# BigBird attention and a swish layer: row-tiled scores, a 0/1 mask product, channels-first AV, row sums by matmul, q and k turned by DMA, in an order written out by hand

## Chip, cores and metric

The kernel runs on one core of a Trainium2 chip. The metric is the device time of one execution in microseconds (us), the median over runs. The engines are TensorE (PE in the profile, its weight loads PEld), VectorE (DVE), ScalarE (ACT), GpSimd (POOL) and SyncE (SP), which here only issues DMAs. SBUF is the on-chip memory, PSUM the memory that TensorE writes its results to, DRAM the memory off the core. Each engine takes its own instructions in program order.

## What is computed

Block-sparse attention over 4 batches, 8 heads, 768 positions and 64 channels, followed by a feed-forward layer (512 to 2048 to 512) on the 3072 tokens:

```python
scores = scale * np.matmul(q, k.transpose(0, 1, 3, 2))
mask = np.abs(blk_i - blk_j) <= window            # blocks of 32, window 1
mask = mask | (blk_i == 0) | (blk_j == 0) | (blk_i == n_blocks - 1) | (blk_j == n_blocks - 1)
...  # and three sampled key blocks per query block
scores = np.where(mask, scores, -1000000000.0)
attn = np.exp(scores - np.max(scores, axis=-1, keepdims=True))
attn = attn / (np.sum(attn, axis=-1, keepdims=True) + 1e-09)
x = np.matmul(attn, v)            # then [B, S, H*D] -> [3072, 512]
h = x @ w_in
out = (h * (1.0 / (1.0 + np.exp(-beta * h)))) @ w_out
```

## The kernel before

**Units of work.** Heads are taken in pairs (`j` = 0 to 3 in each batch `b`). The queries are cut into eight tiles of 256 or 512 columns (`tiles`, L329), and the tiles into seven groups (`groups`, L331) of 256 or 512 tokens. For every tile and pair the attention is computed with keys on the partitions and queries along the row; when a group's tiles are done, its tokens go through the feed-forward layer.

**Loading** (`emit_load` L65). SP issues one plain load each for k, q and v of a pair, 384 KB in fp32, two pairs ahead. Position `s` lies on partition `s // 6`, so a partition reads 1536 contiguous bytes per head. The weights come as eight DMAs on POOL's queue (L143, L147), which cast fp32 to fp16 on the way.

**Preparation** (`emit_prep` L196). VectorE casts k and q to fp16 (L204), TensorE turns each in six 128x128 transposes (L209), and VectorE copies the two heads out of PSUM into four tiles `kA`, `qA`, `kB`, `qB` (L213, L214). The mask sits in the contraction: 24 extra rows hold a one-hot of the block on the key side and 0 or -30000 per block on the query side (L185 to L190), so that a score matmul of 88 rows (head A) or 128 rows (head B) gives masked scores at once. v is cast into `va` with a column of ones (L217).

**Scores and exp** (`step` L227). Per head, two or three key chunks of 128 are multiplied (L234) into a PSUM tile `sc` (two buffers), and ScalarE takes exp of 1024 or 768 columns at a time into `et` (L240): 160 such instructions in all.

**AV** (`av_step` L250). For each 128 queries and each key chunk, 128 columns of `et` are loaded as weights and the 65 columns of `va` stream through (L260): 1152 matmuls, which give queries on the partitions and the row sum in column 64. VectorE takes the reciprocal (L265) and multiplies (L266) into `xst`; TensorE turns that back to channels-first (L274) and VectorE copies it into `xT_sb` (L276).

**Feed-forward** (`moe_steps` L284). A group has 16 `h_step`s, each four matmuls `hp` (L294), a tanh on ScalarE (L299) and a product on VectorE into `g` (L301); then per 128 tokens four `o_step`s of four 512-column matmuls `op` (L313), with the last one's result scaled by ScalarE into `osb` (L318) and stored by SP (L322). `hp`, `op`, `tp` and `xtp` share the three PSUM buffers `mm`.

**Order.** The program order is a list of attention steps per group, with the previous group's feed-forward steps (the backlog) spread evenly between them (L371 to L383); the framework's scheduler may move instructions from that order. A tile's AV steps come after the second score step of the pair that follows.

Of the kernel before, what the change touches and what calls it, by code (L numbers as in the profile page):

```python
# [17 lines left out]
def kernel(  # L18
# [19 lines left out]
    N_TOK = B * S  # L38
# [4 lines left out]
    VW = D + 2  # L43
    NEG = -30000.0

    persist = ctx.enter_context(tc.tile_pool(name="persist", bufs=1))
    stage_pool = ctx.enter_context(tc.tile_pool(name="stage", bufs=3))
    et_pool = ctx.enter_context(tc.tile_pool(name="et", bufs=14))
    work_pool = ctx.enter_context(tc.tile_pool(name="work", bufs=3))
    g_pool = ctx.enter_context(tc.tile_pool(name="g", bufs=2))  # L50


    NVA = 6
    va_tiles = []
    for i in range(NVA):
        va = persist.tile([P, 2, NC, VW], FP16, name=f"va_{i}")
        nc.gpsimd.memset(va[:, :, :, D:VW], 1.0)
        va_tiles.append(va)

    def pair_src(x, b, j):  # L60
        return x[b, 2 * j:2 * j + 2].rearrange("h (p c) d -> p h (c d)", c=NC)

    loaded = {}

    def emit_load(b, j):  # L65
        sts = []
        for name, src in (("k", k), ("q", q), ("v", v)):
            st32 = stage_pool.tile([P, 2, NC * D], FP32, tag=f"{name}st", name=f"{name}st")
            nc.sync.dma_start(out=st32, in_=pair_src(src, b, j))
            sts.append(st32)  # L70
        loaded[(b, j)] = sts

    identity = persist.tile([P, P], FP16, name="identity")

    emit_load(0, 0)
    make_identity(nc, identity)
    ident32 = persist.tile([P, P], FP32, name="ident32")
    nc.gpsimd.tensor_copy(out=ident32[0:16, 0:16], in_=identity[0:16, 0:16])


# [4 lines left out]
    nc.scalar.dma_start(out=sb_i32, in_=sb_lo)  # L85
    beta_sb = persist.tile([N_FFC, P], FP32, name="beta_sb")
    nc.scalar.dma_start(out=beta_sb, in_=moe_beta.rearrange("(c p) -> c p", p=P))

    sb_f32 = persist.tile([NB, 3], FP32, name="sb_f32")
    nc.vector.tensor_copy(out=sb_f32, in_=sb_i32)  # L90


# [10 lines left out]
    onehot = persist.tile([NB, NC, P], FP16, name="onehot")  # L103
    nc.gpsimd.memset(onehot, 1.0)
    nc.gpsimd.affine_select(out=onehot, in_=onehot, pattern=[[1, NC], [NC, P]],
                            compare_op=ALU.is_ge, fill=0.0, base=0,
                            channel_multiplier=-BLK)
    nc.gpsimd.affine_select(out=onehot, in_=onehot, pattern=[[-1, NC], [-NC, P]],
                            compare_op=ALU.is_ge, fill=0.0, base=BLK - 1,
                            channel_multiplier=BLK)  # L110

    mask_blk = persist.tile([NB, NB], FP32, name="mask_blk")
# [3 lines left out]
    for val in (0.0, float(NB - 1)):  # L116
        nc.vector.scalar_tensor_tensor(out=mask_blk, in0=iota_j, scalar=val, in1=mask_blk,
                                       op0=ALU.is_equal, op1=ALU.max)
        nc.vector.scalar_tensor_tensor(
            out=mask_blk, in0=iota_i[:, 0:1].to_broadcast([NB, NB]), scalar=val,  # L120
            in1=mask_blk, op0=ALU.is_equal, op1=ALU.max)
    for r in range(3):
        nc.vector.scalar_tensor_tensor(out=mask_blk, in0=iota_j, scalar=sb_f32[:, r:r + 1],
                                       in1=mask_blk, op0=ALU.is_equal, op1=ALU.max)
    mask16 = persist.tile([NB, NB], FP16, name="mask16")
    nc.vector.tensor_scalar(out=mask16, in0=mask_blk, scalar1=1.0, scalar2=-NEG,  # L126
                            op0=ALU.subtract, op1=ALU.mult)
    oh_flat = onehot.rearrange("j c p -> j (c p)")


    xT_sb = persist.tile([P, NPAIR, N_TOK], FP16, name="xT_sb")
    w_in_sb = persist.tile([P, NPAIR, D_FF], FP16, name="w_in_sb")
    w_out_sb = persist.tile([P, N_FFC, D_MODEL], FP16, name="w_out_sb")
    beta_h_sb = persist.tile([P, N_FFC], FP32, name="beta_h_sb")

    w_in_r = moe_w_in.rearrange("(c p) f -> p c f", p=P)
    w_out_r = moe_w_out.rearrange("(c p) m -> p c m", p=P)

    def gate(w, like):
        nc.gpsimd.tensor_copy(out=w[0:1, 0, 0:1], in_=like[0:1, 0, 0:1])  # L140

    def emit_w_in(i):
        nc.gpsimd.dma_start(out=w_in_sb[:, :, i * 512:(i + 1) * 512],  # L143
                            in_=w_in_r[:, :, i * 512:(i + 1) * 512])

    def emit_w_out(i):
        nc.gpsimd.dma_start(out=w_out_sb[:, i * 4:(i + 1) * 4, :],  # L147
                            in_=w_out_r[:, i * 4:(i + 1) * 4, :])


    sc_pool = ctx.enter_context(
        tc.tile_pool(name="sc_psum", bufs=2, space=bass.MemoryType.PSUM))
    av_pool = ctx.enter_context(
        tc.tile_pool(name="av_psum", bufs=1, space=bass.MemoryType.PSUM))
    mm_pool = ctx.enter_context(
        tc.tile_pool(name="mm_psum", bufs=3, space=bass.MemoryType.PSUM))

    NSET = 5  # L160
    sets = []
    for i in range(NSET):
        four = {}
        for nm in ("kA", "qA", "kB", "qB"):
            four[nm] = persist.tile([P, S], FP16, name=f"{nm}_{i}")
        nc.gpsimd.memset(four["kB"][0:D, :], 0.0)
        nc.gpsimd.memset(four["qB"][0:D, :], 0.0)
        sets.append(four)

    maskx_box = {}  # L170

    def emit_mask():
        ps = mm_pool.tile([P, 512], FP32, tag="mm", name="bet")
        nc.tensor.transpose(out=ps[:, 0:N_FFC], in_=beta_sb, identity=ident32[0:16, 0:16])
        nc.vector.tensor_scalar(out=beta_h_sb, in0=ps[:, 0:N_FFC], scalar1=0.5,
                                scalar2=None, op0=ALU.mult)
        maskx = persist.tile([NB, S], FP16, name="maskx")
        for lo, hi in ((0, 512), (512, S)):
            ps = mm_pool.tile([P, 512], FP32, tag="mm", name="mkx")
            nc.tensor.matmul(ps[0:NB, 0:hi - lo], lhsT=mask16, rhs=oh_flat[:, lo:hi],  # L180
                             start=True, stop=True)
            nc.vector.tensor_copy(out=maskx[:, lo:hi], in_=ps[0:NB, 0:hi - lo])
        maskx_box["m"] = maskx

    def emit_set(i):  # L185
        four, maskx = sets[i], maskx_box["m"]
        nc.vector.tensor_copy(out=four["qA"][D:D + NB, :], in_=maskx)
        nc.gpsimd.tensor_copy(out=four["kA"][D:D + NB, :], in_=oh_flat)
        nc.vector.tensor_copy(out=four["qB"][0:NB, :], in_=maskx)
        nc.gpsimd.tensor_copy(out=four["kB"][0:NB, :], in_=oh_flat)  # L190


    prepared = {}
    n_prep = [0]

    def emit_prep(b, j):  # L196
        kst, qst, vst = loaded.pop((b, j))
        four = sets[n_prep[0] % NSET]
        if n_prep[0] < NSET:
            emit_set(n_prep[0])  # L200
# [216 lines left out]
```

The softmax here doesn't subtract the row's maximum and nothing guards it: scores larger than these inputs give would overflow.

## Time and profile before

| | value |
|---|---|
| median of 3 runs | 339.46 us (339.13 to 339.80) |
| span of the profiled execution | 337.4 us |
| PE busy, matmuls | 298.4 us, 2659 |
| ACT busy | 215.8 us |
| DVE busy | 181.7 us |
| POOL busy | 28.0 us |
| DMA written | 29.78 MB, 20880 packets |
| granted TensorE clock, mean | 0.998 |

The span runs from the first to the last instruction of the profiled execution; the median of the runs is 2.1 us above it. A busy time is the union of an engine's instructions, not their sum. Matmuls are pipelined: the mean duration of one 512-column matmul in the page is 379 ns, while 32 in a row take 7.07 us, 0.22 us from one to the next.

### The profile page before, as it was taken

The numbers are of one execution on the slowest core, as the hardware profiler recorded it, in microseconds if no ns is written. First come the engines' busy times: TensorE is split into PE (matmuls) and PEld (weight loads), VectorE is DVE, ScalarE is ACT, GpSimd is POOL, SyncE is SP. The second block draws the span as 40 slices with busy tenths as digits, with TensorE's granted clock in tenths as the row PEclk, the third lists the DMA queues.
The fourth block names the chain that finished last, engine by engine and source line by source line (L and its number), as shares of the span: only waits on it lengthen the run. The fifth ranks groups of instructions, "written<-read, shape, count | busy, mean of one in ns | idle before, by whom it ended". The sixth has DMA issues, their size and how long they took to land.

```text
span 337.4 us, 6399 instructions
## 1 busy us (share of the span) xinstructions
PE 298.4 (88%) x2659; PEld 172.2 (51%) x2659; DVE 181.7 (54%) x408; ACT 215.8 (64%) x297; POOL 28.0 (8%) x48
## 2 busy tenths in 40 slices
PE   0055589999999999999999999999999999999995
PEld 0034466655555555555566445455455455555662
DVE  3989764543787451557866366115667114561360
ACT  1011389985998545978554989665986756954561
POOL 9994000000000000000000000000000000000000
PEclk9999999999999999999999999999999999999999
DMA  7999994112530340021340000011000010001101
GB/s 242 384 228 225 267 330 179 50 47 80 161 97 11 123 130 33 31 79 64 96 157 31 33 0 2 31 38 58 1 3 0 33 62 33 0 2 62 64 2 62
DMA packets 20880, 29.78 MB, mean 88 GB/s; under 512 B 1380, under 2 KB 17780, under 8 KB 20852
## 3 DMA queue, kind: packets, MB, share of 16 engines
q1 hardware_dynamic: 16512, 25.17, 21.8%
q0 software_dynamic: 4224, 4.19, 7.5%
q8 instruction: 21, 0.34, 0.4%
q14 instruction: 7, 0.06, 0.1%
q10 hardware_dynamic: 116, 0.01, 0.0%
HBM read 27.27 MB, written 6.29 MB: 99 GB/s over the span
## 4 chain that ended last, share of the span: by engine, by line
PE 64%; DVE 16%; ACT 14%; issue 4%; DMA 2%; SPq 0%; ACTq 0%; DVEq 0%
PE op L313 23%; PE hp L294 16%; PE sc L234 12%; PE av L260 9%; ACT et L240 8%; ACT t_sb L299 6%; DVE g L301 4%; PE tp L209 2%; PE xtp L274 2%; DMA qst<-in_q_dram 2%; DVE q_203 L204 1%; DVE va_70 L217 0%; DVE xst L266 0%; DVE qB_157 L214 0%; DVE qB_139 L214 0%
## 5 line engine op out<-in xcount | busy, mean ns | idle before, releaser
L240 ACT ACTIVATE et<-sc 128x1024 f16<-128x1024 f32 (+1 forms) x160 | 146.8, 953 | 80.4 <-PE sc L234 80.2
L313 PE MATMUL op<-w_out_sb,g 128*128 128x512 f16 x384 | 97.0, 379 | 0.1
L294 PE MATMUL hp<-xT_sb,w_in_sb 128*128 128x512 f16 (+1 forms) x448 | 95.6, 348 | 1.0 <-DVE g L301 0.2
L301 DVE SCALAR_TENSOR_TENSOR g<-t_sb,hp 128x512 f16<-128x512 f16 (+1 forms) x112 | 67.1, 610 | 44.9 <-ACT t_sb L299 44.4
L299 ACT ACTIVATE t_sb<-hp,beta_h_sb 128x512 f16<-128x512 f32 (+1 forms) x112 | 69.8, 653 | 12.1 <-PE hp L294 10.9
L294 PEld LDWEIGHTS <-w_in_sb 128*128 128x128 f16 x448 | 42.2, 97 | 35.9 <-issue 1.9
L260 PEld LDWEIGHTS <-et 128*128 128x128 f16 x1152 | 44.2, 99 | 21.6 <-DVE xst L266 10.4
L313 PEld LDWEIGHTS <-g 128*128 128x128 f16 x384 | 34.9, 97 | 33.2 <-DVE qB_163 L214 0.4
L265 DVE RECIPROCAL recip<-av 128x2 f32<-128x2 f32 (+1 forms) x64 | 11.2, 176 | 70.3 <-PE av L260 70.0
L318 ACT ACTIVATE osb<-op 128x512 f32<-128x512 f32 x24 | 14.3, 598 | 23.2 <-PE op L313 19.7
L266 DVE TENSOR_TENSOR xst<-av,recip 128x128 f16<-128x128 f32 (+1 forms) x64 | 22.8, 357 | 1.6
L276 DVE COPY xT_sb<-xtp 128x256 f16<-128x256 f16 (+1 forms) x32 | 11.5, 358 | 14.6 <-PE xtp L274 14.6
L274 PEld LDWEIGHTS <-xst 128*128 128x128 f16 x96 | 6.4, 97 | 12.5 <-DVE xst L266 12.2
L260 PE MATMUL av<-va_70,et 128*128 128x65 f16 x216 | 9.6, 199 | 2.8 <-DVE xst L266 2.7
L234 PE MATMUL sc<-qB_139,kB_138 128*128 128x256 f16 (+1 forms) x48 | 11.6, 344 | 0.5 <-ACT et L240 0.5
L274 PE MATMUL xtp<-identity,xst 128*128 128x128 f16 x96 | 10.9, 222 | 1.0 <-DVE xst L266 0.9
L234 PE MATMUL sc<-qA_137,kA_136 88*128 88x256 f16 (+1 forms) x48 | 11.1, 344 | 0.5 <-ACT et L240 0.3
L180 PE MATMUL mkx<-onehot,mask_121 24*24 24x512 f16 (+1 forms) x2 | 0.8, 506 | 10.3 <-DVE mask_121 L126 10.3
L260 PE MATMUL av<-va_72,et 128*128 128x65 f16 x216 | 9.5, 196 | 0.0
L234 PE MATMUL sc<-qB_145,kB_144 128*128 128x256 f16 (+1 forms) x36 | 8.8, 348 | 0.9 <-ACT et L240 0.9
L234 PE MATMUL sc<-qA_143,kA_142 88*128 88x256 f16 (+1 forms) x36 | 8.7, 350 | 0.6 <-ACT et L240 0.6
L234 PE MATMUL sc<-qB_163,kB_162 128*128 128x512 f16 (+1 forms) x36 | 8.5, 325 | 0.7 <-ACT et L240 0.7
(206 smaller groups left out, 249.4 us busy)
## 6 DMA issues: line engine op xcount, KB each, us to landing
kst<-in_k_dram SPq DMA_DIRECT2D x16, 384.0 KB, 4.7
qst<-in_q_dram SPq DMA_DIRECT2D x16, 384.0 KB, 5.5
vst<-in_v_dram SPq DMA_DIRECT2D x16, 384.0 KB, 5.4
out_dram<-osb SPq DMA_DIRECT2D x24, 256.0 KB, 2.0
w_in_sb<-in_moe_w_in_dram POOLq DMA_DIRECT2D x4, 512.0 KB, 10.1
w_out_sb<-in_moe_w_out_dram POOLq DMA_DIRECT2D x4, 512.0 KB, 21.7
sb_i_95<-in_sampled_blocks_dram ACTq DMA_DIRECT2D x1, 0.3 KB
beta_sb<-in_moe_beta_dram ACTq DMA_DIRECT2D x1, 8.0 KB, 4.5
```

The lines of the kernel that those rows point to most:

```text
L234: nc.tensor.matmul(sc[:, i * n:(i + 1) * n], lhsT=kx[0:rows, (kc0 + i) * P:(kc0 + i + 1) * P], rhs=qx[0:rows, q0:q0 + n], start=True, stop ...
L240: nc.scalar.activation(out=et[:, 0:kn * n], in_=sc[:, 0:kn * n], func=AF.Exp, bias=0.0, scale=SCALE)
L260: nc.tensor.matmul(av[:, qc, :], lhsT=et[:, i * n + qc * P:i * n + (qc + 1) * P], rhs=va[:, hh, kc, 0:D + 1], start=(kc == 0), stop=(kc == ...
L265: nc.vector.reciprocal(out=recip[:, 0:nq], in_=av[:, 0:nq, D])
L266: nc.vector.tensor_tensor(out=xstage[:, 0:nq, hh * D:(hh + 1) * D], in0=av[:, 0:nq, 0:D], in1=recip[:, 0:nq].to_broadcast([P, nq, D]), op= ...
L274: nc.tensor.transpose(out=xtp[:, qc, :], in_=xstage[:, qc, :], identity=identity)
L276: nc.vector.tensor_copy(out=xT_sb[:, j, b * S + q0:b * S + q0 + n], in_=xtp[:, 0:nq, :].rearrange("p c s -> p (c s)"))
L294: nc.tensor.matmul(hp[:, 0:n], lhsT=w_in_sb[:, c, f * P:(f + 1) * P], rhs=xT_sb[:, c, t0:t0 + n], start=(c == 0), stop=(c == NPAIR - 1))
L299: nc.scalar.activation(out=t_sb[:, 0:n], in_=hp[:, 0:n], func=AF.Tanh, bias=0.0, scale=beta_h_sb[:, f:f + 1])
L301: nc.vector.scalar_tensor_tensor(out=g[:, f, 0:n], in0=t_sb[:, 0:n], scalar=1.0, in1=hp[:, 0:n], op0=ALU.add, op1=ALU.mult)
L313: nc.tensor.matmul(op, lhsT=g[:, f, ts * P:(ts + 1) * P], rhs=w_out_sb[:, f, :], start=(f == 0), stop=(f == N_FFC - 1))
L318: nc.scalar.activation(out=osb, in_=op, func=AF.Copy, bias=0.0, scale=0.5)
```

## The change

Nearly the whole kernel is rewritten around the same tiles and groups. The reader needs these parts:

- The framework's scheduler is off (`manual_schedule`); every engine's order is the program's.
- k and q are cast to fp16 by DMAs from DRAM to DRAM on POOL's queue (`emit_load`), in an order where one row holds both heads' 64 channels of a position, then turned by a DMA transpose on SP's queue into `kT` and `qT` (128 channels of a pair by 768 positions, `emit_turn`). v is cast by a DMA into `va`. The first four pairs and the eight weight DMAs are issued one after the other on POOL's queue.
- The mask is a tile `mask01` of 0 and 1 (keys by queries), built once; VectorE multiplies it into `et` after the exp, leaving out the first and last query block, for which every key is allowed.
- Score matmuls contract 64 rows: head 0 in the upper half of the array, head 1 in the lower, each into a PSUM bank of its own. An exp always covers 1024 columns.
- AV has v as weights (64 columns a head) and streams `et`: head 0 gives partitions 0 to 63, head 1 gives 64 to 127, so the result is channels-first.
- Row sums are matmuls with ones as weights, 32 columns of the array for each of four heads (a "couple" is two pairs). VectorE takes the reciprocals, and five DMAs on SP's queue write them to DRAM and read them back, broadcast over 64 partitions each, into `rb`. One VectorE product then writes `xt`.
- The output's scaling moves from ScalarE to VectorE.
- The order: 144 score steps; a couple's sums come 2 steps after its last score step, its AV products 8 and 9 steps after; a group's feed-forward steps are appended one step later and fed at 1.28 us of estimated TensorE work a step (`PACE`), as long as there are any.

```diff
+    ctx.enter_context(tc.manual_schedule())
...
-    et_pool = ctx.enter_context(tc.tile_pool(name="et", bufs=14))
+    kq_pool = ctx.enter_context(tc.tile_pool(name="kq", bufs=6))
+    et_pool = ctx.enter_context(tc.tile_pool(name="et", bufs=26))
...
+        k16 = dram_pool.tile([S, 2, D], FP16, tag="k16", name="k16")
+        q16 = dram_pool.tile([S, 2, D], FP16, tag="q16", name="q16")
+        va = kq_pool.tile([P, 2, NC, D], FP16, tag="va", name="va", bufs=8)
+        for src, dst in ((k, k16), (q, q16)):
+            nc.gpsimd.dma_start(out=dst.rearrange("s h d -> h s d"), in_=src[b, 2 * j:2 * j + 2])
+        nc.gpsimd.dma_start(
+            out=va.rearrange("p h c d -> p (h c) d"),
+            in_=v[b, 2 * j:2 * j + 2].rearrange("h (c p) d -> p (h c) d", p=P))
...
+        for st, dst in ((k16, kT), (q16, qT)):
+            nc.sync.dma_start_transpose(out=dst.unsqueeze(1),
+                                        in_=st.rearrange("s h d -> s (h d)"))
...
+    mask01 = persist.tile([P, NC, S], FP16, name="mask01")
+    for c in range(NC):
+        ps = sc_pool.tile([P, 1024], FP32, tag="sc", name="mk")
...
+    def couple(b, q0, n, j0, xt_off, xt_key):
+        kn = 512 // n
...
+                sc = sc_pool.tile([P, 2, kn, n], FP32, tag="sc", name="sc")
                 for i in range(kn):
+                    for hh in range(2):
+                        nc.tensor.matmul(
+                            sc[:, hh, i, :],
+                            lhsT=kT[hh * D:(hh + 1) * D, (kc0 + i) * P:(kc0 + i + 1) * P],
+                            rhs=qT[hh * D:(hh + 1) * D, q0:q0 + n],
+                            start=True, stop=True)
+                et = et_pool.tile([P, 2, kn, n], FP16, tag="et", name="et")
+                nc.scalar.activation(out=et, in_=sc, func=AF.Exp, bias=0.0, scale=SCALE)
+                lo = BLK if q0 == 0 else 0
+                hi = n - BLK if q0 + n == S else n
                 for i in range(kn):
+                    m = mask01[:, kc0 + i, q0 + lo:q0 + hi]
+                    nc.vector.tensor_tensor(
+                        out=et[:, :, i, lo:hi], in0=et[:, :, i, lo:hi],
+                        in1=m.unsqueeze(1).to_broadcast([P, 2, hi - lo]), op=ALU.mult)
...
+        def sums():
+            dt = av_pool.tile([P, 512], FP32, tag="av", name="dsum")
+            for h in range(nh):
+                for kc in range(NC):
+                    for t in range(4):
+                        nc.tensor.matmul(
+                            dt[32 * t:32 * t + 32, 0:256],
+                            lhsT=sel[:, h, :] if nh == 2 else ones32,
+                            rhs=ets[(t // 2, t % 2, kc)][:, h * 256:(h + 1) * 256],
+                            start=(h == 0 and kc == 0), stop=(h == nh - 1 and kc == NC - 1))
+            r = work_pool.tile([P, 256], FP32, tag="recip", name="recip")
+            for x in range(2):
+                nc.vector.reciprocal(out=r[:, x * 128:(x + 1) * 128],
+                                     in_=dt[:, x * 128:(x + 1) * 128])
+            dr = dram_pool.tile([P, 256], FP32, tag="dr", name="dr")
+            nc.sync.dma_start(out=dr, in_=r)
...
+                    nc.sync.dma_start(out=rb[hh * D:(hh + 1) * D, 0:n],
+                                      in_=src.to_broadcast([D, n]))
...
+        def av(jj):
...
+                at = av_pool.tile([P, 512], FP32, tag="av", name="av")
+                for kc in range(NC):
+                    for hh in range(2):
+                        nc.tensor.matmul(at[hh * D:(hh + 1) * D, 0:n],
+                                         lhsT=va[:, hh, kc, :],
+                                         rhs=ets[(jj, hh, kc)],
                                          start=(kc == 0), stop=(kc == NC - 1))
+                nc.vector.tensor_tensor(out=xt[:, j0 + jj, xt_off:xt_off + n],
+                                        in0=at[:, 0:n], in1=box["rb"][jj][:, 0:n],
+                                        op=ALU.mult)
...
-                    nc.scalar.activation(out=osb, in_=op, func=AF.Copy, bias=0.0, scale=0.5)
+                    nc.vector.tensor_scalar(out=osb, in0=op, scalar1=0.5, scalar2=None,
+                                            op0=ALU.mult)
...
+    LAG_S, LAG_A0, LAG_A1 = 2, 8, 9
...
+    PACE = 1.28
+    def feed(amount):
+        acc = amount + feed.left
+        while backlog and acc >= backlog[0][0] * 0.5:
+            c, fn = backlog.pop(0)
+            fn()
+            acc -= c
+        feed.left = acc if backlog else 0.0
...
+        while n_turned < len(seq) and first_use[n_turned] <= x + 7:
+            emit_turn(n_turned)
+            n_turned += 1
+            if n_turned >= 3 and n_loaded < len(seq):
+                emit_load(n_loaded)
+                n_loaded += 1
...
+        feed(PACE if x < n_steps else 1.0)
```

## The prediction

> **What bounds the kernel now.** I read the page's busy times and slices first, then the chain of waits, the groups by shape, and last the timeline of the tail.
>
> ```profile
> PE 298.4 (88%) x2659; PEld 172.2 (51%) x2659; DVE 181.7 (54%) x408; ACT 215.8 (64%) x297; POOL 28.0 (8%) x48
> ...
> PE   0055589999999999999999999999999999999995
> ...
> ACT  1011389985998545978554989665986756954561
> ...
> PE 64%; DVE 16%; ACT 14%; issue 4%; DMA 2%; SPq 0%; ACTq 0%; DVEq 0%
> ```
>
> TensorE is idle or half idle for 45 us and then busy to the end. The stretch from 100 to 300 us, in equal windows (columns: busy time of PE, PEld, DVE, ACT, POOL), leaves it 3.7 of 200 us:
>
> ```profile
> 100.00:150.00 50.00, 48.54 (x444) 27.06 (x441) 25.86 (x58) 35.38 (x47) 0.00 (x0) 1.00 0.21 70
> 150.00:200.00 50.00, 48.76 (x457) 28.45 (x456) 31.89 (x76) 35.38 (x49) 0.00 (x0) 1.00 0.21 69
> 200.00:250.00 50.00, 49.30 (x420) 25.85 (x420) 23.87 (x50) 36.85 (x48) 0.00 (x0) 1.00 0.06 22
> 250.00:300.00 50.00, 49.70 (x405) 26.55 (x403) 22.86 (x46) 35.97 (x50) 0.00 (x0) 1.00 0.06 22
> ```
>
> Busy is not the same as streaming, so the chain is asked for the true spacing: 32 output matmuls take 6.92 us, 0.216 us for 512 columns, 0.108 for 256.
>
> ```profile
> 326.58 6.92 PE op L313 x32
> ```
>
> So TensorE bounds the kernel, at its streaming rate, and ScalarE is next at 36 of 50 us. The rows that price the rest:
>
> ```profile
> L240 ACT ACTIVATE et<-sc 128x1024 f16<-128x1024 f32 x96 | 97.0, 1046 | 28.9 <-PE sc L234 28.7
> L299 ACT ACTIVATE t_sb<-hp,beta_h_sb 128x512 f16<-128x512 f32 x80 | 55.3, 710 | 10.3 <-PE hp L294 9.2 <-DVE recip L265 1.0
> L301 DVE SCALAR_TENSOR_TENSOR g<-t_sb,hp 128x512 f16<-128x512 f16 x80 | 54.1, 686 | 34.2 <-ACT t_sb L299 33.8
> L301 DVE SCALAR_TENSOR_TENSOR g<-t_sb,hp 128x256 f16<-128x256 f16 x32 | 13.0, 421 | 10.7 <-ACT t_sb L299 10.6
> 14.90 3.15 POOL L143 DMA_DIRECT2D w_in_sb<-in_moe_w_in_dram  x4
> ```
>
> **TensorE's work, part by part.** Removed: by line, the AV matmuls (48.6 us busy), the q/k transposes (16.7) and the transposes back (10.9), 76 us. Scores before: 192 x 0.216 + 192 x 0.108 = 62.2 us. Feed-forward: 704 x 0.216 + 128 x 0.108 = 165.9, unchanged. New: the scores have the same columns in 384 half-height matmuls; run two at a time, 31.1 us. AV has as many columns, two at a time 31.1. Sums: 576 matmuls of 256 columns, four at a time, 15.6. Total 243.7 for 298.4. Whether tiles overlap no row of before shows; the ends are full overlap (243.7) and none (165.9 + 3 x 62.2 = 352.5). I take full overlap, because score tiles have rows and banks of their own and AV tiles columns of their own; the other end is a rival.
>
> **A cost between tiles.** TensorE now alternates each step between tiled and whole-array matmuls. A 512-column matmul lasts 379 ns (page) but its successor starts after 216: if the array empties at a switch, that costs up to 163 ns, else 0, so two switches add 0 to 0.33 us a step. The Trainium skill speaks against this change here: TensorEngine Tiling (Array Packing), section Tiling Modes, says a change of tiling mode, not of tile, drains the engine. By that rule the upper end would hold, which would add some 32 us over 98 mixed steps if TensorE set all of them; without it nothing. The rows say only what an emptying could cost; I use their middle.
>
> **ScalarE.** 144 exps of 1024 (1.01 us each, 97.0 / 96) = 145, tanh 69.8, outputs gone (14.3 us moves): about 215, unchanged.
>
> **VectorE.** Removed by line: casts 21.4 and 9.3, copies 17.6, 17.9 and 5.3, reciprocals 11.2, normalising 22.8, copy back 11.5: 117 us. Left: g 67.1. Added: outputs 24 x 0.686 = 16.5; `xt` 16 x 0.686 + 16 x 0.421 = 17.7; reciprocals: 128x2 takes 170 ns and 128x4 182, so 6 ns an element, 0.93 us for 128, 32 of them 29.8 (0.29 each at the 1.04 ns an element of the g rows, so 9 to 30; I take 30, the row of the same operation). The mask product: g's two rows give 1.04 ns an element and 0.157 fixed, so 960 elements cost 1.15 us at one a cycle; the fp16 copies `kA` (768 elements in 550 ns, fixed part taken off) run at 0.51 ns, so 0.65 us. A wide tile takes 96 of 960, a narrow one 96 of 448 (0.39 or 0.62 us): 100 or 170 us. All operands are fp16 in SBUF, as the fast row's are 16 bit, so I take 100. Total 231, from 181.7.
>
> **The steps.** TensorE a step: scores 0.216, AV and sums 46.7 / 144 = 0.32, feed-forward 1.28: 1.82. Feed-forward's first half (hp) needs 1.5 tanh of 0.69 beside an exp: ScalarE 1.01 + 1.04 = 2.05; VectorE 0.65 + (2 x 0.93 + 2 x 0.69) / 12 + 1.5 x 0.68 = 1.94, in narrow tiles 2.2. The second half (op) is TensorE's, 1.82 to 2.15. I take 1.96 for both (1.82 to 2.1). A step without feed-forward is ScalarE's, 1.01.
> How many of each: tiles end at steps 12, 36, 60, 72, 84, 108, 132, 144, and a group's work is there 10 steps after its last tile. It lasts 13.7 / 1.28 = 10.7 steps for 256 tokens, 27.4 / 1.28 = 21.4 for 512. So after step 12: 10 steps bare, 10.7 fed, 13.3 bare, four times 21.4 fed and 2.6 bare, 2 fed. Fed 98.3 x 1.96 = 192.7; bare 33.7 x 1.01 = 34.0. Then ten positions of 1.0 us of feeding plus some 0.3 of sums and AV, 13; then 27.4 - 2.6 - 10 = 14.9 of the sixth group, and the last as now: hp three in 1.62 us (timeline of the tail), 8.6, op 7.0, last output and its store 3.9: 34.4. Sum 274.
>
> **The start.** Scores now begin at 21.7 us behind VectorE's casts. After the change q of pair 3 is the eleventh DMA on POOL's queue, and step 9 needs it. POOL needs 0.79 us for a DMA of 512 runs (row above); one load has 1536: 0.8 (by instruction) to 2.4 us (by run). In the packet records a 512-byte packet takes 27 ns and a 1536-byte one 65, so 256 bytes some 18; the cast 2048-byte ones take 98. With 96 packets an engine: 1.7 to 9.4 us a load. I take 2.4. So 1 + 11 x 2.4 = 27.4, landing 2.0 (output stores' row), the transpose, then three steps. The transpose has no row: 2.0 by that store, 55 us if each 2-byte element cost a 9 ns packet on 16 engines; its runs are 256 bytes, nearest to the loads (384 KB land in 4.7), so 4. Step 12 ends at 36 (29 with 1.7 and 2.0; 113 with 9.4). The Trainium skill, DMA: Bandwidth & Descriptors, Specifications, asks for 512 bytes or more, below which the engine reads, modifies and writes; these write 128. If that doubled the 2.4, step 12 would end at 63.
>
> **The new wait.** From sums to `rb`: sums 1.3, reciprocals 1.9, store 0.4 + 2.0, four loads 1.6 + 2.0 (issue 0.4 each, landing as the stores): 9.2 us. The window is six steps: 11.8 fed, but 6.1 bare. Some four couples come late by up to 3 us; `xt` then stands at the head of VectorE's queue with mask products and g behind it, for which sums and op matmuls wait. I add 5 (0 to 12). A late turn on SP's queue would hold these DMAs too.
>
> **Sum.** 36 + 274 + 5 = 315 against a span of 337.4; with the 2.1 us between span and median, **317 us**.
>
> **Rivals.**
> - *Everything overlaps, no switch costs:* 29 + 34 + 98.3 x 1.82 + 13 + 34.4 = 289, so 291. For it: TensorE streams without gaps now. Against: three engines within 10% of each other and only three `mm` buffers.
> - *The q/k path starves the start (slower):* place, POOL's queue before step 9. The gain after it is 22 us, so it decides from 11 x (r - 2.4) = 22, r = 4.4 us a load, 46 ns a packet. At the cast row's 98 ns, 9.4 us, 48 loads alone take 451 us, so some 450 to 480. For it: a DRAM target and 128-byte pieces, of which no row exists. Against: 18 ns by the small rows.
> - *Mask product at one element a cycle:* bare steps 1.42 for 1.01 (+14), hp steps 2.43 for 1.96 (49 x 0.47 = +23): 354.
> - *Tiles don't overlap (the change doesn't do what it says):* 0.43 three times a step, 2.57 for 1.96 in 98 fed steps (+60), +10 in the bare ones: 387.
> - *Upper ends of switch and late `rb`:* 98.3 x 0.14 + 7 = +21: 338, about none to slightly slower.
>
> **How the numbers follow.** Forecast (300 to 337) 0.44; full overlap 0.15; no change 0.02; q/k path 0.15; mask 0.08; no overlap 0.07; upper ends and beyond 0.09. Below 0.2%, 0.7 us, a measurement of this kernel can't tell a difference. Faster 0.59, same 0.02, slower 0.39. The range, 291 to 362, takes in full overlap and the slow mask product, and leaves out most of the q/k and no-overlap cases, 0.19 with a little below. The forecast's own is 300 to 337.
>
> **What would show it.** Right: PE busy near 245 to 275; score matmuls in pairs that start together; the mask group near 650 ns at 960 elements; first scores near 15 us, step 12 near 36; ScalarE above 85% in hp stretches. Wrong: score idle time released by the transposes' DMAs; mask product near 1.15 us; VectorE busy above 270; `xt` with long idle before it released by `rb`; sum matmuls spaced 0.1 us apart instead of four together.

## The result, and the profile after

| | before | after |
|---|---|---|
| median | 339.29 us (339.0 to 339.8) | 665.09 us (663.66 to 667.51, 4 runs) |
| ratio, 95% interval | | 1.959 [1.954, 1.965] |
| span of the profiled execution | 337.4 us | 662.6 us |
| PE / DVE / ACT / POOL busy | 298.4 / 181.7 / 215.8 / 28.0 us | 317.0 / 224.5 / 209.2 / 143.4 us |
| packets | 20,880 | 459,407 |
| granted TensorE clock, mean | 0.998 | 0.848 |

The forecast was 317 us, with a range to 362; the kernel takes almost twice its old time. The page of the changed kernel, read in the same order as the page of before (busy times, slices, queues, chain):

```profile
PE 317.0 (48%) x2189; PEld 134.3 (20%) x2189; DVE 224.5 (34%) x414; ACT 209.2 (32%) x261; POOL 143.4 (22%) x63
...
PE   0200001025783242529760603068999252598997
...
DMA packets 459407, 36.36 MB, mean 55 GB/s; under 512 B 446052, under 2 KB 454260, under 8 KB 459380
...
q0 software_dynamic: 422784, 15.01, 57.7%
...
issue 61%; POOL 20%; PE 11%; DMA 5%; DVE 1%; ACT 1%; POOLq 0%
```

TensorE is busy for 48% of the span where it was 88%, and the slices show bursts with gaps from the first tenth to the last. The chain of waits is no longer TensorE's: 81% of it is POOL, either issuing or in time in which it waits for nothing that the profile shows ("issue"). The packet count is 22 times that of before. Where POOL stands is seen in its timeline and in that of SP's queue and TensorE beside it (columns: start, duration, engine, line, what, and in brackets the idle time before it and what ended that):

```profile
1.37 3.88 POOL L73 DMA_DIRECT2D k<-in_k_dram  x1 [0.92 <-POOLq L401]
17.20 1.23 SPq L85 DMA_TRANSPOSE kT<-k  x1
17.50 3.74 POOL L73 DMA_DIRECT2D q<-in_q_dram  x1 [12.26 <-issue]
33.79 1.14 SPq L85 DMA_TRANSPOSE qT<-q  x1
34.10 3.79 POOL L73 DMA_DIRECT2D k<-in_k_dram  x1 [11.37 <-issue]
36.76 1.04 PE L192 MATMUL sc<-qT,kT 64*128 64x256 f16 x8 [5.48 <-DMA qT<-q]
```

The first k load is issued at 1.37; its transpose, which waits for it to land, at 17.20; and POOL's next load at 17.50. So one load takes some 16 us, and POOL starts the next k or q load only when the one before has landed (the load of v goes out at 21.23, right behind that of q, without waiting). This repeats over the whole run: the last of the 32 k/q loads is issued at 551.65, the scores that need it begin at 570.93, and 92 us of ordinary work follow. (551.65 - 1.37) / 31 is 17.8 us a load. It paces the kernel, not the start alone. TensorE's and SP's waits say the same (columns: us in total, times, longest):

```profile
PE sc L192 <- DMA qT<-q: 222.0, 11, 36.8
PE dsum L220 <- DVE xt L255: 67.2, 7, 32.6
```

```profile
SPq L85 <- DMA q<-in_q_dram: 197.1, 13, 15.8
SPq L85 <- DMA k<-in_k_dram: 156.2, 12, 15.5
```

The second line is the same stall once more: SP's queue is in order, and a turn that waits 15 us for its load holds the DMAs of the reciprocals behind it, so `xt` and all that follows it come late. Before the change, the score matmuls' waits (for ScalarE) were 5.1 us in all.

Why a load takes 16 us stands in the packets. The 48 loads of k, q and v are 73,728 pieces of 128 bytes as written, the eight weight loads 4096 packets; that leaves 422,784 - 77,824 = 344,960, and in the packet records all of these are 4 bytes long. 344,960 = 768 x 14 x 32 + 896: for each of the 32 k/q loads, 768 packets on each of 14 engines. The first load alone shows it: between 5.9 and 16.9 us the records hold its 1536 packets of 128 bytes and 10,768 of 4 bytes, 768 x 14 + 16. That leaves two engines for the data, 768 pieces an engine instead of 96. The records do not name the engine of a packet; the split is read from the counts.

### The profile page after: what moved, and what is told of

Read it like the earlier page. It is cut to its first block, busy times and chain, and to the rows that moved or that the text cites. A ratio compares the mean times of both kernels' runs of the same rounds, so it can differ in the third digit from the quotient of the medians.

```text
span 662.6 us, 5603 instructions
## 1 busy us (share of the span) xinstructions
PE 317.0 (48%) x2189; PEld 134.3 (20%) x2189; DVE 224.5 (34%) x414; ACT 209.2 (32%) x261; POOL 143.4 (22%) x63
## 2 busy tenths in 40 slices
DMA packets 459407, 36.36 MB, mean 55 GB/s; under 512 B 446052, under 2 KB 454260, under 8 KB 459380
## 3 DMA queue, kind: packets, MB, share of 16 engines
q0 software_dynamic: 422784, 15.01, 57.7%
## 4 chain that ended last, share of the span: by engine, by line
issue 61%; POOL 20%; PE 11%; DMA 5%; DVE 1%; ACT 1%; POOLq 0%
POOL k L73 9%; POOL q L73 8%; PE op L295 5%; PE hp L274 4%; DMA q<-in_q_dram 2%; POOL va L74 2%; DMA w_in_sb<-in_moe_w_in_dram 2%; PE av L251 1%; PE sc L192 1%; PE dsum L220 0%; ACT t_sb L279 0%; DMA qT<-q 0%; DVE g L281 0%; DVE recip L227 0%; DVE osb L300 0%
## 5 line engine op out<-in xcount | busy, mean ns | idle before, releaser
L198 ACT ACTIVATE et<-sc 128x1024 f16<-128x1024 f32 x144 | 145.1, 1025 | 312.1 <-PE sc L192 312.0
L204 DVE TENSOR_TENSOR et<-et,mask 128x448 f16<-128x448 f16 (+1 forms) x192 | 96.2, 522 | 287.1 <-ACT et L198 286.8
L192 PE MATMUL sc<-qT,kT 64*128 64x256 f16 (+1 forms) x384 | 64.8, 387 | 229.2 <-DMA qT<-q 222.0
L73 POOL DMA_DIRECT2D q<-in_q_dram x16 | 59.7, 3730 | 231.1 <-issue 231.1
L274 PE MATMUL hp<-xt,w_in_sb 128*128 128x512 f16 (+1 forms) x448 | 103.9, 375 | 1.7 <-DVE g L281 1.3
L73 POOL DMA_DIRECT2D k<-in_k_dram x16 | 60.3, 3768 | 172.7 <-issue 170.6
L251 PE MATMUL av<-et,va 128*64 128x256 f16 (+1 forms) x384 | 45.8, 384 | 16.5 <-DVE xt L255 11.3
L255 DVE TENSOR_TENSOR xt<-av,rb 128x256 f16<-128x256 f32 (+1 forms) x32 | 17.7, 554 | 78.6 <-DMA rb<-dr 70.4
L227 DVE RECIPROCAL recip<-dsum 128x128 f32<-128x128 f32 x32 | 28.3, 925 | 10.0 <-PE dsum L220 10.0
L251 PEld LDWEIGHTS <-va 128*64 128x64 f16 x384 | 23.6, 125 | 34.7 <-issue 28.2
L300 DVE TENSOR_SCALAR osb<-op 128x512 f32<-128x512 f32 x24 | 16.5, 688 | 16.2 <-PE op L295 15.6
```

The source lines that it names most:

```text
L73: nc.gpsimd.dma_start(out=dst.rearrange("s h d -> h s d"), in_=src[b, 2 * j:2 * j + 2])
L192: nc.tensor.matmul(sc[:, hh, i, :], lhsT=kT[hh * D:(hh + 1) * D, (kc0 + i) * P:(kc0 + i + 1) * P], rhs=qT[hh * D:(hh + 1) * D, q0:q0 + n], ...
L198: nc.scalar.activation(out=et, in_=sc, func=AF.Exp, bias=0.0, scale=SCALE)
L204: nc.vector.tensor_tensor(out=et[:, :, i, lo:hi], in0=et[:, :, i, lo:hi], in1=m.unsqueeze(1).to_broadcast([P, 2, hi - lo]), op=ALU.mult)
L227: nc.vector.reciprocal(out=r[:, x * 128:(x + 1) * 128], in_=dt[:, x * 128:(x + 1) * 128])
L251: nc.tensor.matmul(at[hh * D:(hh + 1) * D, 0:n], lhsT=va[:, hh, kc, :], rhs=ets[(jj, hh, kc)], start=(kc == 0), stop=(kc == NC - 1))
```

## The experiments

**1. The same load with positions outermost.** Only the order of the dimensions in the DMA's description changes; every byte goes where it went.

```diff
-            nc.gpsimd.dma_start(out=dst.rearrange("s h d -> h s d"), in_=src[b, 2 * j:2 * j + 2])
+            nc.gpsimd.dma_start(out=dst, in_=src[b, 2 * j:2 * j + 2].rearrange("h s d -> s h d"))
```

> The changed kernel with the k and q cast loads written position by position (768 outermost) instead of head by head (2 outermost); same bytes, same 128-byte pieces, same queue. Theory: a load with 2 outermost is worked by 2 DMA engines (768 pieces each at about 21 ns = 16 us) while the other 14 get 4-byte fillers. Then the 344064 fillers vanish, a load lands in 3 to 5 us instead of 16.5, POOL issues the next load at once, step 12 ends near 36 to 45 us, and the total is what the prediction's other terms give, 300 to 325 us. Rival 'small pieces into DRAM are slow by themselves': the pieces are unchanged, so a load stays near 16 us and the total above 600. Rival 'POOL's descriptor work': POOL stays at 3.7 us an issue and a pair still needs some 8.5 us, so step 12 ends near 45 to 50 and the total is 320 to 335.

Measured: 371.84 us (368.3 to 373.04), 1.091 [1.085, 1.098] of before. The page of this kernel:

```profile
PE 301.9 (81%) x2189; PEld 130.6 (35%) x2189; DVE 226.0 (61%) x414; ACT 207.3 (56%) x261; POOL 75.9 (20%) x63
...
q0 software_dynamic: 78720, 13.64, 47.3%
```

78,720 is 73,728 + 4096 + 896: the 4-byte packets of the k/q loads are gone. The first k load lands in 4.8 us instead of 16, and POOL issues a second one at 2.3 us, not at 17.5. So 293 of the 326 us that were lost came from this one line. The first landing came out as expected; the total did not, 47 us above the 325 at the top of the stretch. What is left is still 9% slower than before and 55 us above the forecast; the next experiments take that apart.

**2. Larger pieces.** The loads as in 1, described as 128 pieces of 3 KB read and 1.5 KB written (the interleaving of the heads is left out, so the scores are not those of the reference).

```diff
-            nc.gpsimd.dma_start(out=dst, in_=src[b, 2 * j:2 * j + 2].rearrange("h s d -> s h d"))
+            nc.gpsimd.dma_start(
+                out=dst.rearrange("s h d -> (s h d)").rearrange("(p x) -> p x", p=P),
+                in_=src[b, 2 * j:2 * j + 2].rearrange("h s d -> (h s d)").rearrange("(p x) -> p x", p=P))
```

> As e1_spread, but k and q go to DRAM in their own order, head by head, as 128 pieces of 3 KB read, 1.5 KB written; the turned tiles then hold other elements, so this leaves out the interleaving of the two heads and its output is not the reference's. It prices what the 128-byte pieces still cost after e1_spread. Theory: with 16 engines the pieces are hidden behind the steps except at the start, so 5 to 12 us less than e1_spread (eight loads before pair 3's q, 1 to 1.5 us less each). Rival 'small pieces': several hundred us less than e1_spread.

Measured: 377.72 us in one run, not less than 1. The queue's share falls from 47.3% to 30.4% with 30,080 packets. The pieces became larger still: the k/q loads stand in the packet records as 512 packets of 12,288 bytes, 16 a load, so rows that follow each other on both sides were merged. But k lands in 8.8 us at the median in both (q in 8.3 for 9.9). The small pieces load the engines; that they cost the kernel time is not seen in this one run, and neither the theory's gain nor the rival's was there.

**3. Four outermost, in rows that follow each other.** One DMA a head, described as 4 x 192 rows.

```diff
+            for hh in range(2):
+                nc.gpsimd.dma_start(
+                    out=dst[:, hh, :].rearrange("(a s) d -> a s d", a=4),
+                    in_=src[b, 2 * j + hh].rearrange("(a s) d -> a s d", a=4))
```

> The changed kernel, each k or q load cut into its two heads, and each head written with 4 outermost (4 x 192 positions). Same 128-byte pieces. Theory (the outermost count sets how many DMA engines work): 64 loads of 192 pieces on each of 4 engines, 4-byte fillers on the other 12: 12 x 192 x 64 = 147456 fillers instead of 344064; two such loads, 384 pieces an engine, take about 8 us if they run one after the other, so a pair about 19 us, near what the steps need (16 to 18 us a pair): total 370 to 430 us. Rival 'any load into DRAM in 128-byte pieces from this queue is slow': no clear change of the fillers' count and a total above 600.

Measured: 373.55 us in one run, with 79,232 packets on the queue. The time lies in the expected stretch, but the 147,456 small packets were not there, so this counts against the theory as stated, or the edit did not make what it meant to. 192 rows that follow each other, four times, are one run of 768 on both sides, which can be merged into one dimension. Experiment 4 removes that doubt.

**4. Four outermost that can't be merged.** As 3, with every fourth row in one group, so that neither side has rows that follow each other.

```diff
+            for hh in range(2):
+                nc.gpsimd.dma_start(
+                    out=dst[:, hh, :].rearrange("(s a) d -> a s d", a=4),
+                    in_=src[b, 2 * j + hh].rearrange("(s a) d -> a s d", a=4))
```

> As the changed kernel, but each k/q load is two DMAs, one a head, of every fourth row: outermost size 4, and this time the outer two dimensions can't be merged on either side, as they could in e6_four_engines (rows in order are one run of 768). Theory (a pool-queue load is split by its outermost size, and the engines left over get 4-byte packets): 64 DMAs x 192 pieces x 12 engines = 147,456 more 4-byte packets than the spread load's 900, and the time between: 385 to 480. Rival (only the form with 2 outermost, or with heads outermost, is split badly; e6 was a fair test): no 4-byte packets beyond some 1,400, and 365 to 380 us.

Measured: 425.94 us in one run. The queue's line:

```profile
q0 software_dynamic: 226688, 14.23, 75.3%
```

226,688 less the 77,824 of data and weights leaves 148,864 small packets: the 147,456 foretold and the 1408 that experiment 3 shows too. Four outermost stands between two (665) and 768 (372), with the number of fillers that the rule gives. So on this queue the outermost size sets how many engines work. That rows in order are merged first is the reading of experiment 3 that fits both counts; a merging shows in packet sizes only in experiment 2.

**5. AV one step later.** In 1, the two AV products of a couple and the next couple's sums share one PSUM buffer, `av`, and in narrow tiles they fall on adjacent steps. TensorE's timeline of experiment 1 there:

```profile
156.39 1.49 PE L251 MATMUL av<-et,va 128*64 128x512 f16 x12
158.91 0.84 PE L220 MATMUL dsum<-et,ones 128*32 128x256 f16 x24 [1.03 <-DVE xt L255]
159.68 0.39 PE L192 MATMUL sc<-qT,kT 64*128 64x256 f16 x4
161.71 1.49 PE L251 MATMUL av<-et,va 128*64 128x512 f16 x12 [1.64 <-DVE recip L227]
```

The two rows with brackets wait for VectorE to empty the buffer. The edit:

```diff
-    LAG_S, LAG_A0, LAG_A1 = 2, 8, 9
+    LAG_S, LAG_A0, LAG_A1 = 2, 9, 10
```

> e1_spread with the AV products 9 and 10 steps after a couple instead of 8 and 9; the sums stay 2 after. In narrow tiles a couple's AV then no longer encloses the next couple's sums in the one PSUM buffer that both use, and the reciprocals have one step more. Theory (the rest of the loss is that buffer and the way of the reciprocals): TensorE's idle time before sums released by the xt product (10.5 us) and before AV (17.4 us) shrinks to under 12 together, total 8 to 18 us below e1_spread's 371.8. Rival (the rest is switch costs and the start): under 4 us.

Measured: 365.06 us (364.59 to 367.65), 1.077 [1.073, 1.081], 6.8 us less than 1. TensorE's waits in 1:

```profile
PE av L251 <- DVE xt L255: 10.9, 7, 4.5
PE sc L192 <- DMA qT<-q: 10.6, 2, 7.4
PE dsum L220 <- DVE xt L255: 10.5, 7, 2.3
...
PE av L251 <- DVE recip L227: 6.5, 6, 1.6
```

The 10.5 us of `dsum` are gone, as meant, but the waits of `av` stayed (17.2 us for 17.4) and that for `qT` grew from 10.6 to 18.0 us, so less than that arrives at the end: 6.8 us, between what the theory (8 to 18) and the rival (under 4) expected. The collision is real and worth some 7 us; it is not the main part of the 55.

**6. No row sums.** Experiment 1 without sums, reciprocals, their five DMAs and `rb`; `xt` is multiplied by a constant, so the softmax's normalisation is left out.

```diff
-            dt = av_pool.tile([P, 512], FP32, tag="av", name="dsum")
...
+            pass
...
-                                        in0=at[:, 0:n], in1=box["rb"][jj][:, 0:n],
+                                        in0=at[:, 0:n], in1=rb_const[:, 0:n],
```

> e1_spread without the row sums: no sum matmuls, reciprocals or their DMAs; xt is multiplied by a constant tile, so the normalisation is left out. It prices the whole way of the row sums. By its own work it is 15.6 us of TensorE plus 32 switches of 0.1 and 28 us of VectorE that has room; so if only the work costs, 16 to 22 us less than e1_spread. If its waits cost too (theory: PSUM buffer, DRAM round trip, VectorE's queue), 45 to 65 us less, 307 to 327 us.

Measured: 327.96 us (327.43 to 331.41), 0.968 [0.963, 0.973]: 43.9 us less than 1, just short of the 45 to 65 that the theory of costly waits expected. The sums' own streaming is 15.6 us; twelve groups last 1.49 us where they stream 1.30, and 0.19 more for each of 16 bursts makes it 18.6. So some 25 us were not TensorE's work on the sums. That agrees with 1's waits of TensorE for `xt` and `recip`: 10.9 + 10.5 + 6.5 and 1.8 more of `hp` on `xt`, 29.7 us, of which 6.3 (`av` on `xt`) are there without sums as well. So some 23 us hang on the row sums, for which the prediction had 5. (VectorE, too, is busy for 26 us less here, so the 25 are not waiting for the DMAs alone.)

**7. Weights later.** In 1, pair 3's q waits beside 4 MB of weights: its scores begin at 37.7. Here the weights are issued after pair 3's turn.

```diff
-    for i in range(4):
-        emit_w_in(i)
-    for i in range(4):
-        emit_w_out(i)
...
+            if n_turned == NPAIR:
+                nc.gpsimd.tensor_copy(out=w_in_sb[0:1, 0, 0:1],
+                                      in_=kq[seq[NPAIR - 1]][1][0:1, 0:1])
...
-            if n_turned >= 3 and n_loaded < len(seq):
+            if n_turned >= NPAIR and n_loaded < len(seq):
```

> e1_spread with the eight weight loads issued on POOL's queue only once pair 3's q is turned, instead of before. Theory: the transposes of pair 3 no longer share the DMA engines with the weights (they took 11 us from issue to landing beside 2 to 3 before), so step 12 ends near 28 to 32 us instead of 41, and the total falls by 5 to 12 us. Rival (the weights' own lateness takes it back: the first feed-forward matmul waits): within 3 us of e1_spread.

Measured: 369.93 us (365.73, 368.18, 371.67 and 373.85), 1.090 [1.084, 1.096]: no difference from 1 (368.3 to 373.04) that the runs can tell; a gain of some 5 us, which the two faster ones would give, is not excluded. Step 12 ends at 33 us instead of 41, and the first `hp` begins at 63.9 in both. The timeline between shows why the 8 us do not arrive:

```profile
28.84 1.47 PE L220 MATMUL dsum<-et,ones 128*32 128x256 f16 x24
...
32.51 0.35 SPq L230 DMA_DIRECT2D dr<-recip  x1
...
39.62 2.46 SPq L237 DMA_DIRECT2D rb<-dr  x4
```

The store of the reciprocals is issued at 32.51 and their read, which waits for it, at 39.62: 7.1 us for a store that takes 1.7 at the median. In 1 the same store is issued at 32.53 and its read at 38.72, 6.2 us. In both the weights are on their way at that time; that they are what slows the store is argued, not shown. The first `xt` begins at 45.84 here and at 46.04 in 1, some 16 us after the sums. So it is the way through DRAM that binds the start, in 1 already, and an earlier q of pair 3 gains nothing.

**8. Reciprocals spread by TensorE.** The version that the experiments point to: no way through DRAM. Several things change at once: besides the edit shown, the weights come after pair 2's turn, k/q and v get 8 and 12 buffers for 6 and 8, and loads are issued further ahead.

```diff
-            dr = dram_pool.tile([P, 256], FP32, tag="dr", name="dr")
-            nc.sync.dma_start(out=dr, in_=r)
...
+                bc = mm_pool.tile([P, 512], FP32, tag="mm", name="bc")
+                for h in range(nh):
+                    nc.tensor.matmul(bc[:, h * 256:(h + 1) * 256],
+                                     lhsT=bsel[:, jj, h].rearrange("p a d -> p (a d)"),
+                                     rhs=box["r"], start=True, stop=True)
+                rb = work_pool.tile([P, 512], FP32, tag="rb", name="rb", bufs=4)
+                nc.scalar.activation(out=rb[:, 0:n], in_=bc[:, 0:n], func=AF.Copy,
+                                     bias=0.0, scale=1.0)
...
-    LAG_S, LAG_A0, LAG_A1 = 2, 8, 9
+    LAG_S, LAG_B, LAG_A0, LAG_A1 = 2, 4, 5, 7
...
-        while n_turned < len(seq) and first_use[n_turned] <= x + 7:
+        while n_turned < len(seq) and first_use[n_turned] <= x + 12:
```

> As e1 (371.8 us), but the reciprocals don't go through DRAM: they are written as fp16, and four matmuls of 256 columns with a 0/1 selection matrix spread them over the 128 partitions (0.43 us a couple), ScalarE copies them (2 x 0.5 us a couple); sums, spreading and the two AV products come 2, 4, 5 and 7 steps after a couple; the weights are loaded after pair 2's turn; 8 instead of 6 k/q buffers, 12 instead of 8 V buffers, and the turns are issued 12 steps ahead, so that loads don't wait. My theory (the round trip, its collisions in the one av buffer, and loads that come late behind it make e1's remaining loss): 328 (e4, no sums at all) + about 20 us of sums and spreading - the turns' waits of 15 - the start's 5 to 8: 322 to 340, no wait on xt or recip above 5 us, no wait on qT after the start. Rival (e4 gained because ScalarE and VectorE were unloaded and TensorE had less to do; the round trip itself was hidden): 350 to 372.

Measured: 344.88 us (343.74 to 347.02), 1.016 [1.012, 1.020]: 27 us less than 1 and 17 more than the kernel without sums. How the 27 divide among the way through DRAM and the other edits was not measured. It lies 5 us above the top of the stretch expected and 5 below the rival's. No kind of wait on `xt` is above 3.8 us in all, where 1 has 10.9 and 10.5; 6.2 us of waiting for `qT` remain.

**9. Two steps at a time.** As 8, with the scores of two steps together, so that TensorE changes less often between tiled and whole-array matmuls.

```diff
-        at_step(x)
-        if x < n_steps:
-            steps[x]()
+        for y in (x, x + 1):
+            at_step(y)
+            if y < n_steps:
+                steps[y]()
...
-        feed(PACE if x < n_steps else 1.0)
-        x += 1
+        feed(2 * PACE if x < n_steps else 2.0)
+        x += 2
```

> As e7, but two steps' scores are issued back to back, then the events of both, then twice the feed, so that tiled and whole-array matmuls change over half as often. Theory: a changeover costs about 0.12 us on TensorE (e1: two fed steps took 3.45 us for 3.02 of streaming), 2 in each of 110 to 130 fed steps, half of them gone: 12 to 18 us less than e7. Rival: the changeover is not lost time, or the second score waits for ScalarE's exp of 1.04 us (two score buffers): within 5 us of e7, or slower.

Measured: 340.28 us, 0.999 [0.997, 1.002], 4.6 us less than 8. This is the median of ten runs, nine from 337.83 to 344.15 us and one of 975.65 us, for which the record has no reason. TensorE's busy time in 8 and then in 9:

```profile
PE 299.6 (87%) x2237; PEld 130.5 (38%) x2237; DVE 225.7 (65%) x422; ACT 219.4 (64%) x293; POOL 76.0 (22%) x65
```

```profile
PE 288.1 (85%) x2237; PEld 132.2 (39%) x2237; DVE 226.5 (67%) x422; ACT 218.5 (65%) x293; POOL 76.0 (22%) x65
```

The same 2237 matmuls take 11.5 us less of TensorE. In the order of the matmuls the traces have 278 changes in 8 and 184 in 9, 94 fewer: up to 0.12 us each. The spacing shows the price directly. Four `op` matmuls and then a score matmul, in experiment 1 and in the kernel before, where no tiles are used:

```profile
138.58 1.04 PE L295 MATMUL op<-w_out_sb,g 128*128 128x512 f16 x4
139.55 0.39 PE L192 MATMUL sc<-qT,kT 64*128 64x512 f16 x2
```

```profile
170.92 1.03 PE L313 MATMUL op<-w_out_sb,g 128*128 128x512 f16 x4
171.79 0.82 PE L234 MATMUL sc<-qA_137,kA_136 88*128 88x256 f16 x6
```

From start to start that is 0.97 us after the change and 0.87 before; from the last `op` to the first score it is 0.312 us at the median in 1, 8 and 9, and 0.216 before. So a change costs some 0.10 us, within the 0 to 0.163 that the prediction took. Only 4.6 of the 11.5 us reach the end, within the rival's 5, though its first reason, that the change is not lost time, does not hold. In 9 TensorE waits more on ScalarE and VectorE (`sc` on `et` 6.8 us for 4.7, `bc` on `recip` 4.7 for 2.2).

**10. Even feed.** As 9, with a group's feed-forward spread over the steps until the next group is due.

```diff
+                left = min([y for y in due if y > x + 1] + [n_steps]) - x
+                rate = min(1.6, sum(c for c, _ in backlog) / max(left, 1))
...
-        feed(2 * PACE if x < n_steps else 2.0)
+        feed(2 * rate if x < n_steps else 2.0)
```

> As e8, but the MLP's matmuls are fed evenly until the next group is due, instead of 1.28 us of them a step until they run out. Theory: the bare steps (1.04 us of exp against about 0.8 us of TensorE) are gone, some 40 of 144 steps at 0.25 to 0.4 us: 6 to 15 us less than e8. Rival: ScalarE's exp and TensorE were balanced over the run anyway: within 4 us of e8.

Measured: 333.97 us (332.23 to 336.07), 0.984 [0.979, 0.988]: 6.3 us less than 9, the lower end of what the theory expected, and 1.6% faster than the kernel before (1.2 to 2.1%). This is the one version of the change that beats it while computing all of it. TensorE's slices and its largest waits after the mask is built:

```profile
PE   0365768788999999899999989999989998989995
```

```profile
PE bc L248 <- DVE g L296: 8.1, 11, 1.8
PE bc L248 <- DVE recip L239: 5.3, 6, 2.0
```

The row of nines is that of before. The largest gaps that are left are in the first 80 us, of which TensorE is busy for 50, and before the matmuls `bc`, which wait for one of the three `mm` buffers (8.1 us) and for the reciprocals (5.3).

## Why the prediction was wrong

**The step that failed** stands in "The start": "With 96 packets an engine: 1.7 to 9.4 us a load. I take 2.4." 1536 pieces over 16 engines are 96; over the two engines that the description left, they are 768. The price of a piece, which I had doubted most, was not too low: 2.4 us / 96 is 25 ns, and the measured 16.5 us / 768 is 21, with issue and landing in it (by the packet records the first load's pieces move in 10.7 us, 14 ns each). By my own price the load would have been 19 us, and the 32 loads some 610. The rival "The q/k path starves the start" had the place, POOL's queue, and its condition (from 4.4 us a load), but it, too, drew its price from the piece and stopped at 9.4 us a load and 480 us; it got 0.15. And where I costed a queue by issue time alone, POOL issued no further k or q load until the one before had landed.

The Trainium skill has the rule, in DMA: Bandwidth & Descriptors, Rules for kernel authors: the slowest dimension of the access pattern sets how many engines work, so an outermost size below 16 confines the DMA to at most that many. The same page's section Why a DMA increments its semaphore by 16 and not by 1 says that it looks at the patterns as the instruction carries them, which fits experiment 3, if the two dimensions had merged by then. The runs agree with it at sizes 2 (665.09 us), 4 (425.94) and 768 (371.84), and the counts of 4-byte packets do. I weighed another rule of that page (Specifications), on pieces below 512 bytes; experiment 2, with packets of 12,288 bytes, gained nothing.

**Mis-sized: the new wait.** The prediction named the way from sums to `rb` and gave it 5 us (0 to 12). Experiment 1 shows some 23 us of waits that hang on it, experiment 6 some 25 beyond TensorE's own work. Two things were left out. The single `av` buffer ties sums, AV and the next couple's sums together, so a late `rb` stops TensorE by way of `xt`, at once, in narrow tiles (experiment 5, 6.8 us). And the DMAs were priced at a quiet time: in the start, beside weights, the store took 6.2 us in experiment 1 and 7.1 in experiment 7, and not 2.0.

**The start without that.** Step 12 was to end at 36; in experiment 1 it ends at 41, since q of pair 3 lands beside the weights. What I did not see is that the end of step 12 decides little: experiment 7 brings it to 33 and `hp` begins no earlier.

**Right.** Tiles overlap fully: two 512-column score matmuls in 0.39 us, six such pairs of AV in 1.49, twelve groups of four sums in 1.49 (timeline of the changed kernel):

```profile
172.63 0.39 PE L192 MATMUL sc<-qT,kT 64*128 64x512 f16 x2
```

```profile
191.45 1.49 PE L251 MATMUL av<-et,va 128*64 128x512 f16 x12
```

The mask product runs at the faster of the two rates weighed (0.656 us for 960 elements, taken 0.65), the reciprocal costs 0.925 us (taken 0.93), VectorE is busy 224.5 us (231), ScalarE 209.2 (about 215), a transpose lands in 4.1 to 4.3 us in experiment 1 (4). From the page's groups of the changed kernel:

```profile
L227 DVE RECIPROCAL recip<-dsum 128x128 f32<-128x128 f32 x32 | 28.3, 925 | 10.0 <-PE dsum L220 10.0
```

**The sum.** From 317 to the 371.84 of experiment 1 are 55 us. The new wait took 23 to 25 where 5 stood, so 18 to 20 are its. The changes between tiles were mis-sized too: the trace of experiment 1 has 271 of them, some 27 us of TensorE at 0.10 each, where the sum held 14 (98.3 x 0.14). TensorE's busy time is 301.9 us where 245 to 275 were to show it right; experiments 9 and 10 get 11 us of the end back from the order of the steps alone. Step 12 ends 5 us late, of which experiment 7 shows little at the end. How much of the 27 reached the end, and how the rest divides among bare steps, ScalarE and a TensorE at half its clock in the first 70 us (last section), was not measured in one piece and stays open.

## What to carry to other kernels

Before pricing a DMA by its pieces, write down the access pattern on both sides, merge what can be merged, and read the outermost size: on POOL's queue it decided over how many engines the pieces were spread, and the packet count of the page, divided by the pieces asked for, shows at once when it went wrong. A value that goes through DRAM only to be spread over partitions costs its latency beside whatever else is moving; a 0/1 matmul of 256 columns does it on the core. And a wait is priced by what shares a buffer with it, not by the window of the one that waits.

## What the runs showed of the hardware that was not expected

- By the packet counts, engines without a share in a load on POOL's queue got 4-byte packets, as many as a working engine had pieces: 768 on each of 14 in the changed kernel; the count for 12 engines and 192 pieces fits in experiment 4.
- With such a load under way POOL issued the load of v behind it, but not the next k or q load: 11.4 to 14.6 us of "issue" wait before 28 of the 31 that follow the first, where experiment 1 issues a second load 1.03 us after the first. What POOL waits for there, no trace shows.
- The granted clock fell when TensorE worked in bursts. In windows of 30 us of the changed kernel (columns: window, its length, busy time and instructions of PE, PEld, DVE, ACT and POOL, granted clock, DMA share, GB/s):

```profile
170.00:200.00 30.00, 24.85 (x196) 12.68 (x194) 19.21 (x37) 20.12 (x30) 7.70 (x3) 0.99 0.97 56
200.00:230.00 30.00, 8.55 (x74) 3.64 (x76) 7.18 (x11) 8.57 (x9) 8.54 (x3) 0.56 0.74 60
```

  It is 0.99 where TensorE is busy for 25 of 30 us, and 0.56 where it waits; in experiment 10 it is 1.00 from 39 us on. The Trainium skill, TensorE: Matmul & The Clock Gate, What's actually happening, has the clock halved after an idle window of about 3.4 us, which fits these rows, and the trace's stretches at half clock, which last 3.41 us or a multiple of it (only the last one, cut off by the end, does not).
- A profile's full clock at the start was not a measurement. In the changed kernel the clock's slices show nines from the start on, but the trace's first clock record begins at 172 us, and time without a record is shown as full clock. The same work tells more (timeline of the changed kernel):

```profile
38.49 0.61 PE L192 MATMUL sc<-qT,kT 64*128 64x256 f16 x4 [0.69 <-ACT et L198]
540.05 0.61 PE L192 MATMUL sc<-qT,kT 64*128 64x512 f16 x2
542.51 0.39 PE L192 MATMUL sc<-qT,kT 64*128 64x512 f16 x2
```

  At 540.05 the record says half clock, at 542.51 full; at 38.49, for as many columns, the time is that of half clock. In the kernel before, whose first record begins at 43 us, six score matmuls of 256 columns take 1.49 us at 21.69 and 0.82 at 171.79. So the means of 0.848 and 0.998 are too high, and experiment 1, whose scores take 0.61 us up to 68.65 and whose first record begins at 70 us, starts at half clock too.
- A change between tiled and whole-array matmuls cost some 0.10 us (experiment 9).
